# One core, attention and two feed-forward blocks in float32: Strassen's scheme for the first batch and for y, w1 and w2 gone through once

## The chip, the cores and the metric

The kernel runs on one core of one Trainium2 chip. The metric is the device time of one execution in microseconds, the median of three runs. A core has TensorE (PE, with its weight loads as PEld), VectorE (DVE), ScalarE (ACT), GpSimd (POOL) and SyncE (SP), which here issues every DMA. A profiled execution gives the trace from which all rows below are taken.

## What is computed

Four batches of 576 tokens, eight heads of 64, go through three blocks, one after the other:

```python
def _attn_ref(q, k, v):            # window 128, causal, a slope per head
    scores = np.where(mask, scale * np.matmul(q, k.transpose(0, 1, 3, 2)) + bias[None], -1000000000.0)
    attn = softmax(scores)
    return np.matmul(attn, v)

def _moe_ref(x, w1, w2, w3, w_out):   # x 2304x512, w1, w2 512x1024, w3 1024x1024, w_out 1024x512
    a = x @ w1
    b = x @ w2
    h = a * b @ w3
    return h @ w_out

def _moe2_ref(x, w_in, w_out):        # w_in 512x2048, w_out 2048x512
    h = np.maximum(x @ w_in, 0.0)
    return h * h @ w_out
```

## The kernel before

**A planner orders everything.** The kernel consists of tasks (`add(name, rank, where, fn, deps, takes, gives)`), each a few instructions, with an assumed cost on each engine that may run it. `Plan.run` goes through an assumed time: among the tasks that can start within 0.1 us of the earliest it takes the one with the lowest rank, and puts it at the end of its engine's list. So the order on every engine, SyncE's DMA queue among them, is fixed when the kernel is built. `hold` describes a tile: a tag with so many buffers (the table at line 288) and how many tasks must give it back. Gates (tasks of cost 0) close one pool of memory and open another.

**Precision.** A float32 matmul is done as three fast ones: every operand is split into a high and a low part (a copy, and a difference on VectorE or POOL), and `mm3` (lines 194 to 197), `mm3s` and `add_sab` (1080 to 1082) multiply high by high, high by low and low by high. The weights come in as words of 64 bits; `conv_g`, `conv_s`, `conv_m` (lines 328 to 348) turn 1024 of them per partition into float32: a Prelu on ScalarE, a shift on VectorE or ScalarE, a shift with OR on VectorE.

**Strassen's scheme.** Where it is used, a product of 2 x 2 blocks takes seven block products (P1 to P7) in place of eight. Four sums of blocks are made of each operand (`combine`), then seven high and low parts; the seven products accumulate in three PSUM banks, from which VectorE and ScalarE take four results.

**The stages.**
- Attention: sixteen pairs of heads, `add_pair`. Beside it TensorE multiplies w3 by w_out (`p_w34`, L659, 128 matmuls of 512 columns) once and for all, so that y = (a b) w34. The w1, w2 words of eight blocks `fi` of 128 columns are converted (`add_weights`), split for batch 0, and stored in `m_scr["c"]`.
- Batch 0 (`NS = 1`), plain: `add_ab` makes a and b (L195 to L197, output from x and wu), `l_gf` multiplies them to g, `l_gh` and `l_gl` split g, and `add_y` multiplies by w34 (output from gt and wu). The x of batch 0 stays on the chip.
- Batches 1 to 3: x was stored in `x_scr` and is loaded back; `add_xops` makes Strassen's seven operands of it, `add_wmake` loads a block of w1, w2 from `m_scr["c"]` and makes its seven (18 times in all: 8, 5 and 5, since three blocks are kept from batch to batch), `add_sab` makes a, b and g of one block of one batch: 42 matmuls of 288 columns. Then `add_y`, plain, 192 matmuls a batch, from g on the chip; the result goes to `y_scr`.
- r: y by w_in with ReLU, Strassen, 24 groups of 42 matmuls of 384 columns (`add_r`), results to `s_scr`.
- o: squares by w_out, Strassen, nine groups of 168 matmuls of 256 columns (`add_o`), results to `out`.

The words of w_in and w_out of the second block are converted between these (`add_merge`, sixteen of them) and stored in `m_scr`, from where `add_words2` takes them.

## Time and profile before

| | |
|---|---|
| median of three runs | 819.62 us (817.3, 819.62, 821.97) |
| span of the profiled execution | 817.3 us |
| TensorE matmuls | 6724, busy 802.8 us |
| VectorE | 1368 instructions, busy 614.4 us |
| ScalarE | 999 instructions, busy 466.5 us |
| POOL | 69 instructions, busy 57.8 us |
| DMA | 143.99 MB |

Busy times are unions of what an engine shows as running. Matmuls are pipelined, so their busy time says less than their starts do. An idle time is put down to what ended it. A line number can be that of a helper (L200 and L260 are copies on ScalarE and VectorE, L203 is the difference that makes a low part); then the tiles tell what was done.

### The profile page before, as it was taken

Reading aid. Unit: us, or ns where it says so; the run is one execution under the profiler, and the core shown is the slowest. Engines: PE = TensorE matmul, PEld = TensorE weight load, DVE = VectorE, ACT = ScalarE, POOL = GpSimd, SP = SyncE. Lnnn points to the kernel's source line nnn. Section 1 sums busy time; section 2 is a strip of 40 time slices with the busy share of each in tenths; the row PEclk is TensorE's granted clock in tenths of the full one; section 3 lists DMA queues with packets and bytes.
Section 4 is the critical chain, followed back from the end, with each engine's and each line's share of the span. In section 5 each row is a group of like instructions: output and inputs, shape, how many; then the busy total and the mean of one; then the engine's idle time right before and its main releaser. Section 6 shows DMA issues by size and latency. Waiting matters only on the chain. (4 is left out here: it accounts for less than half of the span.)

```text
span 817.3 us, 17269 instructions
## 1 busy us (share of the span) xinstructions
PE 802.8 (98%) x6724; PEld 746.9 (91%) x6724; DVE 614.4 (75%) x1368; ACT 466.5 (57%) x999; POOL 57.8 (7%) x69
## 2 busy tenths in 40 slices
PE   8999999999999999999999999999999999999998
PEld 6665666599999899999999999999999999999998
DVE  6999999956798996896499475733766897667762
ACT  6998888723233442341244476755786785566531
POOL 1000000000001000110040130000222100000000
PEclk9999999999999999999999999999999999999999
DMA  9998989788623642102132457666873755554200
GB/s 224 279 312 262 274 279 279 274 314 263 216 84 109 205 173 84 68 16 84 44 112 101 160 183 263 235 221 210 246 239 134 224 148 155 143 151 135 85 27 33
DMA packets 98402, 143.99 MB, mean 176 GB/s; under 512 B 11024, under 2 KB 75024, under 8 KB 96272
## 3 DMA queue, kind: packets, MB, share of 16 engines
q1 hardware_dynamic: 98320, 142.90, 55.1%
q8 instruction: 52, 0.85, 0.4%
q14 instruction: 30, 0.25, 0.1%
HBM read 98.44 MB, written 44.43 MB: 175 GB/s over the span
## 5 line engine op out<-in xcount | busy, mean ns | idle before, releaser
L196 PE MATMUL g<-gt,wu 128*128 128x288 f32 x256 | 75.7, 296 | 0.0
L195 PE MATMUL g<-gt,wu 128*128 128x288 f32 x256 | 75.6, 295 | 0.0
L197 PE MATMUL g<-gt,wu 128*128 128x288 f32 x256 | 75.4, 295 | 0.0
L443 ACT ACTIVATE e<-e,st 128x128 f32<-128x128 f32 (+1 forms) x144 | 62.3, 435 | 9.0 <-DVE st L435 8.6
L659 PE MATMUL g<-raw 128*128 128x512 f32 x128 | 62.9, 599 | 1.1 <-DVE wu L203 1.0
L200 ACT ACTIVATE D<-xa 128x384 f32<-128x384 f32 (+1 forms) x99 | 45.1, 455 | 30.4 <-PE xa L1133 26.6
L1192 DVE TENSOR_TENSOR D<-xb,D 128x384 f32<-128x384 f32 (+1 forms) x62 | 32.2, 520 | 38.3 <-PE xb L1133 19.0
L1080 PE MATMUL al<-x,wc 128*128 128x288 f32 x192 | 57.5, 299 | 1.1 <-ACT d L200 1.1
L1082 PE MATMUL al<-x,wc 128*128 128x288 f32 x192 | 56.7, 295 | 0.0
L1081 PE MATMUL al<-x,wc 128*128 128x288 f32 x192 | 56.6, 295 | 0.0
L200 ACT ACTIVATE ye<-g 128x288 f32<-128x288 f32 x32 | 13.1, 411 | 73.4 <-PE g L197 66.0
L203 DVE TENSOR_TENSOR ww<-fq,ww 128x1024 fp32r<-128x1024 f32 x35 | 42.5, 1222 | 16.2 <-ACT ww L200 15.9
L200 ACT ACTIVATE ww<-fq 128x1024 fp32r<-128x1024 f32 x35 | 36.9, 1057 | 25.6 <-PE xb L1133 12.0
L1264 ACT ACTIVATE D<-D 128x384 f32<-128x384 f32 x73 | 37.5, 522 | 23.4 <-DVE D L1192 22.4
L868 DVE TENSOR_TENSOR st<-st 128x256 f32<-128x256 f32 (+1 forms) x105 | 41.2, 427 | 9.6 <-DMA st<-m_scrc 5.6
L196 PEld LDWEIGHTS g<-gt,wu 128*128 128x128 f32 x256 | 48.3, 189 | 0.0
L197 PEld LDWEIGHTS g<-gt,wu 128*128 128x128 f32 x256 | 48.2, 188 | 0.0
L195 PEld LDWEIGHTS g<-gt,wu 128*128 128x128 f32 x256 | 48.1, 188 | 0.0
L200 ACT ACTIVATE d<-al 128x288 f32<-128x288 f32 x71 | 28.8, 410 | 32.1 <-PE al L1082 22.9
L503 PEld LDWEIGHTS t<-ident,e 128*128 128x128 f32 x208 | 23.7, 142 | 22.8 <-ACT pt L200 9.7
L435 DVE CUSTOM_DVE_ANT_0 e<-s,bw 128x192 f32<-128x192 f32 (+1 forms) x128 | 40.5, 351 | 1.0 <-PE s L467 0.7
L467 PEld LDWEIGHTS s<-qk 64*64 64x64 f32 x768 | 28.3, 137 | 13.6 <-issue 5.8
(287 smaller groups left out, 2790.9 us busy)
## 6 DMA issues: line engine op xcount, KB each, us to landing
s_scr<-D SPq DMA_DIRECT2D x96, 192.0 KB, 2.1
u<-in_w2io_dram SPq DMA_DIRECT2D x32, 512.0 KB, 6.4
fo<-s_scr SPq DMA_DIRECT2D x20, 512.0 KB, 5.4
qk<-in_qk_dram SPq DMA_DIRECT2D x32, 288.0 KB, 5.5
st<-m_scrc SPq DMA_DIRECT2D x18, 512.0 KB, 3.9
raw<-in_w3t_dram SPq DMA_DIRECT2D x8, 1024.0 KB, 10.2
raw<-in_w_dram SPq DMA_DIRECT2D x8, 1024.0 KB, 7.4
fq<-s_scr SPq DMA_DIRECT2D x16, 512.0 KB, 5.2
```

The costliest lines, as they stand in the source:

```text
L195: nc.tensor.matmul(o, wh, xh, start=start, stop=False)
L196: nc.tensor.matmul(o, wh, xl, start=False, stop=False)
L197: nc.tensor.matmul(o, wl, xh, start=False, stop=stop)
L200: nc.scalar.activation(out=o, in_=i, func=ACTF.Copy)
L203: eng.tensor_tensor(out=o, in0=a, in1=b, op=ALU.subtract)
L435: nc.vector.tensor_tensor_reduce(out=part_of(m, x, rows), in0=ps, in1=bias, op0=ALU.add, op1=ALU.min, scale=-0.125, scalar=3.0e38, accum_o ...
L443: nc.scalar.activation(out=e, in_=e, func=ACTF.Exp, bias=st[:, 0, x:x + 1], scale=-1.0, accum_out=st[:, 1, x:x + 1],)
L659: nc.tensor.matmul(gw[fi], wl, wr, start=c == 0, stop=c == 7)
L868: ENG[e].tensor_tensor(out=o, in0=a, in1=b, op=op)
L1080: nc.tensor.matmul(o, wh, xh, start=start and c == 0, stop=False, skip_group_check=True)
L1081: nc.tensor.matmul(o, wh, xl, start=False, stop=False, skip_group_check=True)
L1082: nc.tensor.matmul(o, wl, xh, start=False, stop=c == 1, skip_group_check=True)
```

## The change

- All sixteen pairs of attention store x in `x_scr`. All four batches are loaded back, and the operands of all four (28 tiles of 576 columns, high and low) are on the chip at the same time, in three pools: xA (open from the start: batch 0 and one of batch 1), xB (open when all of attention's x is stored, gate "sp"), xC (open when w3 w_out is stored, gate "gp").
- w1, w2 are converted and combined once per block. The loop goes over pairs of blocks, in them over the batches, in those over the two blocks. `m_scr["c"]` and the eighteen remakes are gone.
- Batch 0 goes through `add_sab` like the others. The first a, b product waits for "pp": all of x copied out of PSUM.
- g goes to `g_scr` in DRAM (two stores per block and batch), w3 w_out to `w_scr`.
- y is a stage behind a, b, by Strassen's scheme: `add_wy` loads w3 w_out and makes its seven operands of 1024 columns, `add_gops` loads g of one batch (four loads) and makes its seven (in halves of 576 columns), `add_y` does 84 matmuls of 288 columns for each batch and half of the outputs. `add_seven` is the scheme shared with a, b.
- All sixteen `add_merge` are tied to a, b blocks, from the fourth on. Working tiles of r and o (st, s0, fo, yB and the operands of P1, P2) become xA, whose eight tiles have 1152 columns.

```diff
-RANK = dict(w34=3, vv=20, w0=-15, c0=0, cj=3, h0=-40, w12=35.93, w12s=7.96, w12l=7.68, mg=500, mgs=4, yl=8, yn=0, hs=7)
+RANK = dict(w34=3, vv=20, w0=-15, c0=0, cj=3, h0=-40, hs=7, w12=60, wa=7, wl=9, wb=0, x0=20, mg=4, mgs=1.6, wo=1126, gg=-3, yq=1142)
...
-            u=11, u34=4, wo=4, qk=2, v=2, e=NE, s=NPS, t=1, pt=NE, a=5 - NPS, g=2, asb=2, gf=2, gt=8, ye=2,
-            al=2, be=2, ga=2, d1=2, d2=2, d4=2, gq=8, pl=1, xm=1, xt1=1, xt2=1, yA=14, yB=6, s0=1, t2a=1, t2b=1, v6=6, st=2, xa=2, xb=2, xc=2, D1=2, D2=2, D4=2, D3=1, fo=4, fq=5, ww=4,
-            **{f"x_{k}": 1 for k in range(7)},
+            u=11, wo=4, qk=2, v=2, e=NE, s=NPS, t=1, pt=NE, a=5 - NPS, g=2, pl=1, sg=2,
+            d1=2, d2=2, d3=1, d4=2, xA=8, xB=12, xC=8, xa=2, xb=2, xc=2,
+            yA=14, t2a=1, v6=6, D1=2, D2=2, D4=2, D3=1, E1=2, fq=5, ww=4,
...
-    def l_w34h(fi, e):
-        if fi % 2 == 0:
-            w34[fi // 2] = slot("u34")
-        copy(e, w34_part(fi)[:, 0], gw[fi])
-
-    def l_w34l(fi, e):
-        s = w34_part(fi)
-        sub(nc.vector, s[:, 1], gw.pop(fi), f(s[:, 0]))
+    def l_w34(fi, e):
+        t = su.tile([128, 512], F32, tag="sg", bufs=2, name="sg")
+        copy(e, t, gw[fi])
+        gw[fi] = t
+
+    def t_w34(fi):
+        nc.sync.dma_start(out=w_scr[fi], in_=gw.pop(fi))
...
+    def open_pp():
+        psb.close()
+        q = late.enter_context(tc.tile_pool(name="ps_p", bufs=1, space=PSUM, reuse_waits="tile"))
+        pool.update(xa=q, xb=q, xc=q)
...
+    def open_sp():
+        att.close()
+        pool["xB"] = xbs.enter_context(tc.tile_pool(name="xB", bufs=1, side="right", reuse_waits="tile"))
...
+        pool["xC"] = xcs.enter_context(tc.tile_pool(name="xC", bufs=1, reuse_waits="tile"))
+
+    def open_q1():
+        xbs.close()
+        q = q1.enter_context(tc.tile_pool(name="q1", bufs=1, side="right", reuse_waits="tile"))
+        pool.update(yA=q, t2a=q, D1=q)
+
+    def open_ph():
+        xcs.close()
+        dds.close()
+        q = late.enter_context(tc.tile_pool(name="ph", bufs=1, reuse_waits="tile"))
+        pool.update({k: q for k in ("v6", "E1", "D2", "D3", "D4")})
...
+        key = ("w12", fi)
+        add_words(key, rank - RANK["wa"], "u", 8, 3, RANK["wl"] - RANK["wa"], after)
...
+    XA = {(0, P): "xA" for P in SP_}
+    XA.update({(1, P): "xA" if P == 1 else "xB" for P in SP_})
+    XA.update({(2, P): "xC" if P == 4 else "xB" for P in SP_})
+    XA.update({(3, P): "xC" for P in SP_})
+    ROOM = {"xA": [], "xB": ["sp"], "xC": ["gp"]}
...
+        add("lx" + z, rank - 3, {"dma": w_dma(1180)}, lambda e: ld(), [f"sx{4 * b + k}" for k in range(K1)] + prev, ["xm0" + z, "xm1" + z], keep=1)
...
+    def add_seven(z, tag, mms, w, deps, gives, rank, last, y):
...
+        for x, (P, nm, start, dep) in enumerate((
+            (1, "xa", True, []), (2, "xc", True, []), (6, "xa", False, ["d1" + K]), (7, "xb", True, []),
+            (5, "xa", False, ["d2" + K]), (3, "xa", False, ["d4" + K]), (4, "xb", False, ["c22" + K]),
         )):
-            part = A_AT[P][0]
-            add(f"sP{P}_{z}", 1000 + rank + 0.1 * x, {"pe": 6 * w_mm(HALF)}, lambda e, P=P, nm=nm, start=start: prod(P, nm, start),
-                [f"xol{P}_{b}", f"wl{part}c{fi}{w0}"] + [d for d in dep] + ([f"sP1_{last}"] if P == 1 and last else [])
-                + {6: [f"sP1_{z}"], 5: [f"sP6_{z}"], 3: [f"sP5_{z}"], 4: [f"sP7_{z}"]}.get(P, []),
-                take, [f"xo{b}{P}", f"w{part}c{fi}{w0}"])
+            add(f"{tag}{P}_{z}", 1000 + rank + 0.1 * x, {"pe": w}, lambda e, P=P, nm=nm, start=start: prod(P, nm, start),
+                deps(P) + dep + ([f"{last}"] if P == 1 and last else [])
+                + {2: [f"{tag}1_{z}"], 7: [f"{tag}1_{z}"], 6: [f"{tag}1_{z}"], 5: [f"{tag}6_{z}"], 3: [f"{tag}5_{z}"], 4: [f"{tag}7_{z}"]}.get(P, []),
+                [nm + K] if start else [], gives(P))
...
+            add("c12" + K, -20, w_copy(HALF, True), lambda e: cp("d3", e), [f"{tag}3_{z}"], ["d3" + K], ["xa" + K])
+            for nm, c in D.items():
+                add(f"sy{c}{z}", -15, {"dma": w_dma(147)}, lambda e, nm=nm, c=c: y(c, sb.pop((K, nm))), [f"c{c}{K}"], [], [nm + K])
...
+        add_seven(
+            z, "sP", mms, 6 * w_mm(HALF), lambda P: [f"xol{P}_{b}", f"wl{A_AT[P][0]}c{fi}", "pp"],
+            lambda P: [f"xo{b}{P}", f"w{A_AT[P][0]}c{fi}"], rank, last, None,
+        )
...
+        def st(hf, nm):
+            nc.sync.dma_start(out=g_scr[b][fi][:, HALF * hf:HALF * hf + HALF], in_=sb.pop((K, nm)))
+
+        for hf, nm in ((0, "d2"), (1, "d4")):
+            add(f"sg{b}{hf}{fi}", -15, {"dma": w_dma(147)}, lambda e, hf=hf, nm=nm: st(hf, nm), [f"g{hf}{z}"], [], [nm + K])
...
+    def add_wy(rank):
+        for i in range(2):
+            hold(f"ym{i}", "u", 100)
+        hold("ysx", "xA", 6)
+
+        def ld(i):
+            t = wm[i] = new("u", [128, 4, 512])
+            nc.sync.dma_start(out=t, in_=w_scr[4 * i:4 * i + 4].rearrange("k p n -> p k n"))
+
+        for i in range(2):
+            add(f"lw{i}", rank - 3, {"dma": w_dma(1048)}, lambda e, i=i: ld(i), [f"sw{4 * i + k}" for k in range(4)] + ([f"lw{i - 1}"] if i else [f"whbc{NF1 - 1}"]), [f"ym{i}"], keep=0)
+        M = lambda i: wm[i % 2][:, :, 256 * (i // 2):256 * (i // 2) + 256]
+
...
+    GA = {(b, P): (("xB" if P in (1, 2, 6, 7, 5, 3) else "xA") if b % 2 == 0 else "xC" if P in (1, 2, 6, 7) else "xB" if b == 1 else "xA") for b in range(B) for P in SP_}
...
+        for x, i in enumerate((0, 1, 3, 2)):
+            add(f"lg{i}{z}", rank - 1 + 0.1 * x, {"dma": w_dma(590)}, lambda e, i=i: ld(i),
+                [f"sg{b}{i % 2}{fi}" for fi in range(4 * (i // 2), 4 * (i // 2) + 4)] + ([f"gc3_{b - 1}"] if b else []), [f"gm{i}{z}"])
...
+        for i, (dp, tk, gv) in enumerate((
+            (["lg0" + z, "lg1" + z], [s0], [m[0], m[1]] + [s0]), (["gc0" + z, "lg3" + z], [s1], [m[3], s0, s1]),
+            (["gc0" + z, "lg3" + z], [], [m[1], m[3]]), (["gc1" + z, "lg2" + z, "gl50" + z, "gl51" + z], [], [m[2], s0, s1]),
+        )):
+            add(f"gc{i}{z}", rank + (0, 0.1, 0.2, 0.5)[i], w_tt(4 * HALF), lambda e, i=i: combine("B", i, M, S_, e), dp, tk, gv)
...
+            return [
+                (*(wy[P][:, h, k, 128 * c:128 * c + 128] for h in range(2)), *(go[b, P, k // 2][:, h, k % 2] for h in range(2)))
+                for k in range(4)
+            ]
...
+    add("pp", 0, {"gate": 0.0}, lambda e: open_pp(), [f"xh{g_}_{m}" for g_ in range(2) for m in range(4 * B)])
+    add("sp", 0, {"gate": 0.0}, lambda e: open_sp(), [f"sx{m}" for m in range(4 * B)])
+    add("gp", 0, {"gate": 0.0}, lambda e: open_gp(), [f"sw{i}" for i in range(NF1)])
+
     g = 100
-    order = list(range(NF1))
-    at_w = {}
+    last = None
+    sabs = []
     for b in range(B):
-        if b < NS:
-            for hf in range(2):
-                for i in range(NF1):
-                    add_ab(b, hf, i, g)
-                    g += 1
-                for i in range(K1):
-                    add_y(b, hf, i, g + (hf and RANK["yl"] * (i >= RANK["yn"])))
-                    g += 1
-            continue
-        FO[b] = order
-        at_w[b] = order[-NKEEP:]
-        order = order[:-NKEEP - 1:-1] + order[:-NKEEP]
-    last = None
-    g0 = g
-    for b in range(NS, B):
-        made = b == NS
-        if made:
-            prev = []
-        prev_x = [f"xol{P}_{b - 1}" for P in SP_] if b > NS else []
-        add_xops(b, 1000 + g0 + 20 * (b - NS) - 13, prev_x)
-        for x, fi in enumerate(FO[b]):
-            r = 1000 + g + 1.5 * x
-            kept = b + 1 < B and fi in at_w[b]
-            if b > NS and fi in at_w[b - 1]:
-                w0 = b - 1
-            else:
-                w0 = b
-                add_wmake(fi, b, 1 + kept, r - 6, prev)
-                prev = [f"whbc{fi}{b}"]
-            add_sab(b, fi, g, w0, last)
-            last = f"{b}{fi}"
-            g += 1
-        for i in range(K1):
-            for hf in range(2):
-                add_y(b, hf, i, g + RANK["yl"] * (i >= RANK["yn"] and b < B - 1))
+        add_xops(b, 1000 + g + 2 * b - RANK["x0"], [f"xc3_{b - 2}"] if b > 1 else [])
+    for p in range(NF1 // 2):
+        for x in range(2):
+            add_wmake(2 * p + x, 1000 + g + x - 6, B, [f"sP1_{RANK['wb'] + x}{2 * p - 2}"] if p > 1 or p and x else [])
+        for b in range(B):
+            for x in range(2):
+                add_sab(b, 2 * p + x, g, last)
+                last = f"sP1_{b}{2 * p + x}"
+                sabs.append(last)
                 g += 1
+    add_wy(RANK["wo"])
+    for b in range(B):
+        add_gops(b, 1000 + g + RANK["gg"] + 4 * b)
+    for b in range(B):
+        for c in range(2):
+            add_y(b, c, g, last)
+            last = f"Y1_{b}{c}"
+            g += 2
...
+    add("q1", 0, {"gate": 0.0}, lambda e: open_q1(), [f"Y{P}_{b}1" for b in range(lb) for P in SP_ if GA[b, P] == "xB"])
+    add("ph", 0, {"gate": 0.0}, lambda e: open_ph(),
+        [f"sy{k}{lb}{c}" for k in ("11", "12", "21", "22") for c in range(2)] + [f"Y{P}_{lb}1" for P in SP_])
...
+        add_merge(k, m, 1080 + x, prev + [sabs[min(31, int(RANK["mg"] + RANK["mgs"] * x))]])
```

## Rows read from the trace of the kernel before

**Rows 1.** Busy times by stage: window, length, engine busy (instructions), clock, DMA share, GB/s.

```profile
0.00:160.80 160.80, 153.66 (x1988) 101.50 (x1988) 144.30 (x598) 135.62 (x438) 5.53 (x22) 0.99 0.91 273
167.00:456.00 289.00, 285.83 (x2132) 283.35 (x2133) 227.44 (x449) 103.68 (x203) 23.33 (x19) 1.00 0.38 130
```

In the order PE, PEld, DVE, ACT, POOL.

**Rows 2.** Timeline of TensorE: start, duration, line, output and inputs.

```profile
166.71 0.22 PE L543 MATMUL a<-pt,v 64*64 64x64 f32 x1
166.86 0.40 PE L195 MATMUL g<-x,wu 128*128 128x288 f32 x1
...
454.07 0.29 PE L197 MATMUL g<-gt,wu 128*128 128x288 f32 x1
...
456.46 0.29 PE L197 MATMUL g<-gt,wu 128*128 128x288 f32 x1
456.59 0.34 PE L1131 MATMUL xa<-yA,u 128*128 128x384 f32 x1
...
457.12 0.34 PE L1131 MATMUL xa<-yA,u 128*128 128x384 f32 x1
```

**Rows 3.** Busy times in slices of 20 us, columns as in rows 1.

```profile
280.00:300.00 20.00, 19.38 (x142) 18.89 (x142) 19.58 (x37) 11.62 (x20) 1.45 (x1) 1.00 0.35 132
...
340.00:360.00 20.00, 19.57 (x145) 19.09 (x144) 19.17 (x40) 10.93 (x23) 6.19 (x5) 1.00 0.01 5
...
380.00:400.00 20.00, 20.00 (x153) 20.00 (x152) 10.79 (x20) 5.54 (x12) 0.00 (x0) 1.00 0.20 65
```

**Rows 4.** Groups of instructions up to 165 us; then tiles wu and x there.

```profile
L345 DVE SCALAR_TENSOR_TENSOR raw<-raw 128x1024 uint32<-128x1024 uint32 x20 | 24.4, 1222 | 0.5
L339 DVE TENSOR_SCALAR raw<-raw 128x1024 uint32<-128x1024 uint32 x16 | 10.9, 693 | 0.1
L200 ACT ACTIVATE pt<-t 128x512 f32<-128x512 f32 x46 | 27.2, 592 | 9.1 <-PE t L503 8.0 <-ACT e L443 1.0
L330 ACT ACTIVATE raw<-raw 128x1024 f32<-128x1024 f32 x20 | 23.1, 1160 | 0.0
L200 ACT ACTIVATE pt<-a 128x256 f32<-128x256 f32 (+1 forms) x33 | 8.4, 324 | 1.1 <-PE a L543 1.1
...
0.00:165.00 165.00, 3.55 (x24) 3.24 (x24) 20.09 (x23) 5.84 (x9) 0.99 0.91 273
...
0.00:165.00 165.00, 3.55 (x24) 3.24 (x24) 3.53 (x12) 3.00 (x12) 0.99 0.91 273
```

A group has its count, busy time, mean duration in ns, and the idle time before it with what ended that. The windows of a tile have PE, PEld, DVE, ACT.

**Rows 5.** Groups of instructions from 167 to 456 us; then tiles wc and gt there.

```profile
L868 DVE TENSOR_TENSOR st<-st 128x256 f32<-128x256 f32 x72 | 27.5, 419 | 6.0 <-DMA st<-m_scrc 5.6
L1103 DVE TENSOR_TENSOR d<-be,d 128x288 f32<-128x288 f32 x48 | 21.5, 453 | 4.3 <-ACT d L200 2.7 <-PE be L1082 1.3
L203 DVE TENSOR_TENSOR gt<-d,gt 128x288 fp32r<-128x288 f32 x39 | 16.9, 455 | 1.0
L1109 DVE TENSOR_TENSOR d<-d,d 128x288 f32<-128x288 f32 x23 | 12.2, 534 | 0.7
L203 DVE TENSOR_TENSOR x<-xm,x 128x576 fp32r<-128x576 f32 x12 | 8.8, 751 | 0.0
L203 POOL TENSOR_TENSOR gt<-d,gt 128x288 fp32r<-128x288 f32 x9 | 7.8, 870 | 49.3 <-DVE gt L260 32.5 <-ACT gt L200 16.8
L200 ACT ACTIVATE x<-xm 128x576 fp32r<-128x576 f32 x11 | 7.3, 681 | 1.1 <-PE al L1082 0.8 <-PE be L1082 0.3
...
167.00:456.00 289.00, 140.34 (x1008) 135.58 (x1008) 48.08 (x53) 13.98 (x16) 7.84 (x3) 1.00 0.38 130
...
167.00:456.00 289.00, 105.34 (x764) 102.77 (x765) 38.36 (x98) 8.32 (x19) 7.78 (x9) 1.00 0.38 130
```

**Rows 6.** DMA up to 165 us in all; issues with size and time to landing.

```profile
DMA packets 22150, 44.98 MB, mean 273 GB/s; under 512 B 6261, under 2 KB 12405, under 8 KB 20076
...
s_scr<-D SPq DMA_DIRECT2D x96, 192.0 KB, 2.1
```

**Rows 7.** Waits of ScalarE from 637 us to the end: total, times, longest.

```profile
ACT fq L1305 <- DMA fq<-s_scr: 10.6, 10, 2.1
```

More of the change, by code (lines that the diff above doesn't have):

```diff
@@ L206, in fused_kernel @@
     y_scr = dram.tile([K1, 128, NT], F32, name="y_scr")
+    g_scr = [dram.tile([NF1, 128, S], F32, name=f"g_scr{b}") for b in range(B)]
+    w_scr = dram.tile([NF1, 128, DM], F32, name="w_scr")
     TN = 384
@@ L755, in p_y @@
-    def p_y(b, hf, oi, part):
-        if part == 0:
-            yo[b, hf, oi] = ps_g.tile([128, 512], F32, tag="g", name="g")[:, 0:HALF]
-        o = yo[b, hf, oi]
-        fs = (FO[b] if b >= NS else range(NF1))[4 * part:4 * part + 4]
-        for x, fi in enumerate(fs):
-            w = w34[fi // 2][:, :, (fi % 2) * 512 + oi * 128:(fi % 2) * 512 + (oi + 1) * 128]
-            g = gt[b, hf, fi]
-            mm3(o, w[:, 0], w[:, 1], g[:, 0], g[:, 1], part + x == 0, part == 1 and x == 3)
-    def l_y(b, hf, oi, e):
-        t = gp[0].tile([128, HALF], F32, tag="ye", bufs=2, name="ye")
-        copy(e, t, yo[b, hf, oi])
-        yo[b, hf, oi] = t
@@ L796, in fused_kernel, with new @@
+    def new(tag, shape, dt=F32):
+        return (wp if tag == "u" else pool[tag]).tile(shape, dt, tag=tag, bufs=plan.caps[tag], name=tag)
     A_AT = {1: "a0", 2: "a1", 3: "b2", 4: "a3", 5: "b0", 6: "b1", 7: "a2"}
@@ L1005, in hi @@
             def hi(e, part=part, w=w, o=o):
[L1006 to L1007 removed]
+                t = wc[fi, part] = new("u", [128, 2, w], F32R)
+                copy(e, t[:, 0], full()[:, o:o + w])
             def lo(e, part=part, w=w, o=o):
[L1010 to L1013 removed]
@@ L1070, in prod @@
         def prod(P, nm, start):
             if start:
-                sb[z, nm] = ps_p[0].tile([128, 512], F32, tag=nm, bufs=plan.caps[nm], name=nm)[:, 0:HALF]
-            o = sb[z, nm]
-            part = A_AT[P][0]
-            i = 256 * int(A_AT[P][1])
-            w, x = wc[fi, w0, part], xo[b, P]
-            for c in range(2):
-                wh, wl = (w[:, h, i + 128 * c:i + 128 * c + 128] for h in range(2))
-                xh, xl = (x[:, h, HALF * c:HALF * c + HALF] for h in range(2))
+                sb[K, nm] = new(nm, [128, 512])[:, 0:HALF]
@@ new lines, in add_y, with mms, y @@
+    def add_y(b, c, rank, last):
+        z = f"{b}{c}"
+        def mms(P):
+            return [
+                (*(wy[P][:, h, k, 128 * c:128 * c + 128] for h in range(2)), *(go[b, P, k // 2][:, h, k % 2] for h in range(2)))
+                for k in range(4)
+            ]
+        def y(k, t):
+            i, h = int(k[0]) - 1, int(k[1]) - 1
+            t0 = b * S + h * HALF
+            nc.sync.dma_start(out=y_scr[c + 2 * i, :, t0:t0 + HALF], in_=t)
+        add_seven(
+            z, "Y", mms, 12 * w_mm(HALF), lambda P: [f"gl{P}{q}_{b}" for q in range(2)] + [f"ywl{P}"],
+            lambda P: [f"go{b}{P}{q}" for q in range(2)] + [f"wy{P}"], rank, last, y,
+        )
@@ L1356, in prod @@
             return ([f"ol{P}{t}"] + [f"wl{part}o{m}" for m in range(NM)],
-                    [f"ow{P}{t}"] + [f"w{part}o{m}" for m in range(NM)], lambda o, start, P=P, **kw: p_o(t, P, o, start, **kw))
+                    owns[t, P] + [f"w{part}o{m}" for m in range(NM)], lambda o, start, P=P, **kw: p_o(t, P, o, start, **kw))
         def fin(z):
```

596 lines of the change are left out of this document (267 added, 329 removed).

## Prediction

> **What bounds the kernel now.** I read the table of stages first [rows 1]. Up to 160.8 us (attention, with w3 w_out on the side) VectorE is busy 144.3 us (0.90), ScalarE 135.6 us (0.84), and DMA has a share of 0.91. TensorE's 153.7 us there are pipelined latencies and mislead, as the next view shows. From 167 to 456 us TensorE is busy 285.8 of 289 us and VectorE only 227.4 (0.787). So there are two regimes: an attention stage that VectorE and ScalarE set, and then 650 us that TensorE sets.
>
> The second view is the timeline of TensorE [rows 2]. Its starts tell what a matmul of 288 columns costs: 454.07 to 456.46 is eighteen intervals, 0.132 us each, not the 0.30 us that one lasts. The last P V product of attention starts at 166.71, the first matmul of the r stage at 456.59. Between them lie 2136 of the 2160 matmuls of 288 columns that the code has (384 for a, b of batch 0, 1008 for Strassen's a, b, 768 for y); the other 24 have run inside attention, in tile wu of [rows 4]. 2136 x 0.132 = 282.0 of 289.7 us, so the holes are 7.7 us. By slices of 20 us [rows 3]: where VectorE works 10.8 us, 153 matmuls fit; where it works 19.2 or 19.6 us, 145 or 142. A dense VectorE costs TensorE some nine matmuls, 1.2 us in 20.
>
> **The change part by part.** All working is on the profiled span of 817.3 us; the median of the runs is 819.6, so 2.3 is added at the end.
>
> *Matmuls.* By the code, batch 0 goes from 2 x 8 x 2 x 12 = 384 to 8 x 42 = 336, and y from 4 x 2 x 4 x 24 = 768 to 4 x 2 x 84 = 672: 144 fewer of one width, 19.0 us. After the end of attention 2016 stand in place of 2136: 120 x 0.132 = -15.8 us (the other 24 ran inside attention, which the next term contains).
>
> *Attention stage.* Off it go, of VectorE: eight of the OR steps (9.8), eight shifts (5.5), everything into wu (20.1: high and low parts of w1, w2, low parts of w3 w_out) and the low parts of x (3.5) [rows 4], 38.9 us; of ScalarE eight Prelu steps and one copy, 10.3. On it comes what the first products of a, b need. The operands of x for batch 0 are four sums and seven differences at 0.75 us and seven copies at 0.68 [rows 5]: 8.3 and 4.8 us. Three sums and one operand of batch 1 (it lies in xA) are 3.0 and 0.7. A block of w1, w2 costs VectorE 0.69 + 1.22 + 4 x 0.42 + 1.22 + 0.92 = 5.7 us and ScalarE 1.16 + 1.16 + 0.87 = 3.2 (the parts of 768 scaled from 1024) [rows 4, 5]; two of them are 11.5 and 6.4. VectorE goes from 144.3 to 128.2, ScalarE from 135.6 to 137.2; their sum from 279.9 to 265.4, a factor of 0.948, which puts the end of attention from 166.9 to 158. Without the added work the factor is 230.7 / 279.9 = 0.824: 138 us. The added work has the later rank, so attention runs ahead of it, but it must be there before the first product: I take 152 us (-14.9). DMA forbids little more: 45.0 MB [rows 6] less 14.7 (w1, w2 in and back out, four w2io loads) plus 7.8 (more of x out, x in for two batches, w3 w_out out, two blocks in) is 38.1 MB, at 273 GB/s 140 us, the lower bound. Upper bound: 167, if the chain of a pair of heads and not the engines sets the pace.
>
> *Gates.* The new products wait for "pp", all of x copied out of PSUM, where the old ones waited for batch 0 alone. The last three copies take 0.32 us of ScalarE each [rows 4], and their semaphores: +1.5 us (0 if w3 w_out has matmuls left to cover it, 5 if the first weights are late too). The operands in xB wait for "sp", the stores of x; a store lands in some 2.1 us [rows 6], and batch 1 is due only two blocks (84 x 0.132 = 11 us) later: covered. On SyncE's queue 90 transfers are new (64 stores and 16 loads of g, 10 for w3 w_out); a store whose g is late holds the loads of weights behind it, and TensorE waits for those.
>
> *VectorE between attention and r.* Away: 40 of 72 sums for w1, w2 (16.8), of the 48.1 us into wc all but sixteen differences (31.0), everything into gt (38.4), fifteen products a b of batch 0 at 0.45 (6.8) [rows 5]: 93.0 us. To it: eight more blocks of a, b with four additions or products at 0.45 and one at 0.53 (18.8), words of w1, w2 (15.3), 24 additions for y at 0.45 (10.9), eleven steps of 1024 for w3 w_out (13.4), five w2io conversions that now come early (9.6), and the operands of g, four times four sums of 1152 (1.37, scaled from 1.22 for 1024) and 14 differences of 576 (0.75): 64.0 us. Together 132.0. Less what is made in attention (two blocks 11.5, batch 1's 3.0), VectorE goes from 227.4 to 251.9 us. TensorE needs 2016 x 0.132 = 266.1, so VectorE's share rises from 0.79 to 0.95 of that: every slice is a dense one. Fourteen slices at 1.2 us are 16 us of holes in place of 7.7: +8 us (0 if POOL and ScalarE take the surplus; 20 if the joints stall too).
>
> *Joints.* From a, b to y: before its first seven products are through, y needs all operands of w3 w_out and those of g for batch 0. Both can begin when the last block of batch 0 is done, six blocks (33 us) before the end, and VectorE has 14.1 us of a, b, 13.4 and 16 us to do: 43.5 us of work in 33 + 11 us. It fits with nothing over, and is within the +8. From y to r: "ph" waits for the last y store (2.1 us); products 1, 2, 6, 7 of the first r block, 24 matmuls that start every 0.176 us [rows 2], 4.2 us, cover it. In r and o no matmul changes; the five w2io conversions only leave.
>
> *Sum:* 817.3 - 14.9 - 15.8 + 1.5 + 8.0 = 796.1, and with 2.3 for the median **798 us**.
>
> **The rivals.**
> *Attention not shortened.* It ends at 167 because pairs are bound by their chain. For: ScalarE keeps its 137 us. Against: ScalarE's idle time is 9.1 us, put down to transposes, ahead of the copies behind them [rows 4], and VectorE is at 0.90. 798 + 15 = 813.
> *Short attention, no new holes.* It ends at 140, and VectorE keeps up: 798 - 12 - 8 = 778. For: VectorE's work fits into 266 us. Against: the slices of rows 3.
> *POOL is no relief.* The planner may hand differences of g, x and the weights to POOL. For: POOL takes 0.87 us for the difference that VectorE does in 0.455, and VectorE's product out of SBUF has a mean of 0.534 against 0.453 for the sums that read PSUM [rows 5]: handing over 20 differences gives VectorE 9 us and, if it is held meanwhile, takes up to 17, so that the holes grow by 8 more: 806. Against: POOL does only 19 steps in this stretch now [rows 1]. The Trainium skill, "SBUF — State Buffer", section "SBUF: two separate sides", has this as a rule: the two share a port pair as an exclusive lock, and a VectorE instruction with two SBUF inputs is held for the whole of a POOL instruction that reads SBUF. By that rule the sum is 806, without it 798; no row here shows one instruction held by another.
> *Slower: VectorE takes the bound between attention and r.* It must then wait at each joint for g's way through DRAM, as it waits for TensorE now. At its present density of 0.787 the 251.9 us last 320 us; r would begin at 152 + 1.5 + 320 = 473.5 instead of 456.6, 17 us late: 837. It decides from a density below 251.9 / 303.1 = 0.83. For: every difference of g now stands behind the store of its last f block and a load. Against: in attention VectorE holds 0.90, and in two slices of rows 3 0.96 and 0.98.
> *The o stage starves.* Its loads and operands leave pools of their own (fo, st) for xA, eight tiles of which a step takes six, so that loads start later. ScalarE's longest wait for such a load is 2.1 us now, and covered [rows 7]. If each of eight steps lost 2.1 us: 798 + 17 = 815.
>
> **How the numbers follow.** Forecast (790 to 805) 0.38; short attention without holes 0.18; attention not shortened 0.14; POOL 0.08; o starves 0.08; slower 0.14. A measurement of this kernel tells 0.5% (4.1 us) from no change. Below 815.5 us lie the first four and a little of the fifth: faster 0.79; the rest of the fifth and the lower edge of the slower case: same 0.08; slower 0.13. The range, 779 to 816, takes in the bounds of attention and of the holes one at a time, and leaves out the slower case and the corner of the fast one where both ends meet.
>
> **What would show it.** Right: the last P V product near 152 us; 2016 matmuls of 288 columns from there to the first of 384 columns, in some 282 us, at 0.132 each; VectorE above 0.88 there; r to the end still 361 us. Wrong: P V ending at 165 or later; TensorE waiting above 5 us at "pp", before the first y product or before r; VectorE's sums waiting for loads of g; r and o together longer than 365 us.

## The result, and the profile after

| | before | after |
|---|---|---|
| median (lowest to highest) | 819.62 us (817.3 to 821.97) | 806.28 us (804.9 to 812.59) |
| ratio, 95% interval | | 0.9848 [0.9807, 0.9889] |
| span of the profiled execution | 817.3 us | 810.8 us (of 812.59) |

The change is faster by 1.5%. Forecast were 798 us and faster; 806.3 lies inside the range, 8 us above the forecast. The profiled execution is the longest of its kernel, so a second profile of the kernel after (a_again, below) stands beside it. Three stretches answer to the three terms of the sum; their ends are read from TensorE's timeline.

| | before | after | difference | a_again | difference | forecast |
|---|---|---|---|---|---|---|
| start to last P V product | 166.71 | 167.70 | +1.0 | 165.42 | -1.3 | -14.9 |
| to the last matmul of 288 columns | 289.75 | 275.21 | -14.5 | 276.24 | -13.5 | -6.3 |
| to the end | 360.84 | 367.89 | +7.1 | 365.74 | +4.9 | 0 |
| sum | 817.3 | 810.8 | -6.5 | 807.4 | -9.9 | -21.2 |

The middle forecast is -15.8 + 1.5 + 8.0. That the time still lies inside the range is in part luck, since errors of opposite sign stand in the sum: attention got hardly shorter, the holes that were feared did not come, and r and o, for which nothing was forecast, got longer.

Busy times by stage, after (columns as in [rows 1], which they answer):

```profile
0.00:167.70 167.70, 159.03 (x2046) 106.35 (x2046) 132.71 (x571) 142.16 (x462) 12.19 (x25) 0.96 0.83 249
167.80:438.80 271.00, 266.96 (x1996) 264.50 (x1993) 233.75 (x374) 146.03 (x263) 25.46 (x17) 1.00 0.69 223
```

VectorE did lose work in attention, 144.3 to 132.7 us, but the stage didn't end earlier. Between attention and r VectorE's share rose from 0.787 only to 0.863, not to 0.95. The timeline of TensorE after, which answers [rows 2]:

```profile
167.69 0.22 PE L513 MATMUL a<-pt,v 64*64 64x64 f32 x1
167.84 0.40 PE L929 MATMUL xa<-xA,u 128*128 128x288 f32 x1
...
437.22 0.29 PE L929 MATMUL xa<-xA,u 128*128 128x288 f32 x1
...
438.68 0.30 PE L931 MATMUL xa<-xA,u 128*128 128x288 f32 x1
438.81 0.34 PE L1125 MATMUL xa<-yA,u 128*128 128x384 f32 x1
...
442.91 0.29 PE L931 MATMUL xb<-xA,u 128*128 128x288 f32 x1
443.04 0.34 PE L1125 MATMUL xc<-yA,u 128*128 128x384 f32 x1
```

The first product of a, b starts 0.15 us after the last P V product, as it did before [rows 2]: the gate "pp" costs nothing. From 437.22 to 438.68 lie eleven intervals of 0.133 us, the price of a matmul as before. Six matmuls of r run ahead of the last 24 of y. So in the 275.2 us stand 2016 x 0.1327 = 267.5 and 1.1 for the six, and 6.6 us of holes; before, 2136 x 0.1328 = 283.7 of 289.75, 6.1 of holes.

### The profile page after: what moved, and what is told of

Same layout as the page of the kernel before. It is cut to its first block, busy times and chain, and to the rows that moved or that the text cites. A ratio compares the mean times of both kernels' runs of the same rounds, so it can differ in the third digit from the quotient of the medians.

```text
span 810.8 us, 17310 instructions
## 1 busy us (share of the span) xinstructions
PE 791.7 (98%) x6582; PEld 735.0 (91%) x6582; DVE 612.7 (76%) x1291; ACT 510.7 (63%) x1090; POOL 67.9 (8%) x65
## 5 line engine op out<-in xcount | busy, mean ns | idle before, releaser
L196 ACT ACTIVATE d<-xa 128x288 f32<-128x288 f32 x128 | 52.2, 409 | 97.4 <-PE xa L931 93.3
L196 ACT ACTIVATE D<-xa 128x384 f32<-128x384 f32 (+1 forms) x91 | 41.8, 462 | 30.0 <-PE xa L1127 26.4
L931 PE MATMUL xa<-xB,u 128*128 128x288 f32 x192 | 56.8, 296 | 0.0
L929 PE MATMUL xa<-xB,u 128*128 128x288 f32 x192 | 56.8, 296 | 0.0
L930 PE MATMUL xa<-xB,u 128*128 128x288 f32 x192 | 56.1, 292 | 0.0
L716 DVE TENSOR_TENSOR xA<-xA 128x256 f32<-128x256 f32 (+2 forms) x74 | 47.7, 669 | 3.0 <-DMA xA<-g_scr 1.5
L950 DVE TENSOR_TENSOR d<-xb,d 128x288 f32<-128x288 f32 x80 | 36.2, 452 | 15.2 <-ACT d L196 10.8
L473 PEld LDWEIGHTS t<-ident,e 128*128 128x128 f32 x208 | 24.4, 144 | 23.6 <-ACT pt L196 11.2
L437 PE MATMUL s<-qk 64*64 64x128 f32 (+2 forms) x768 | 37.5, 293 | 5.0 <-issue 2.1
L473 PE MATMUL t<-ident,e 128*128 128x128 f32 x208 | 36.8, 291 | 1.7 <-ACT pt L196 1.3
L930 PEld LDWEIGHTS xa<-xB,u 128*128 128x128 f32 x192 | 36.5, 190 | 0.0
L929 PEld LDWEIGHTS xa<-xB,u 128*128 128x128 f32 x192 | 36.1, 188 | 0.0
L931 PEld LDWEIGHTS xa<-xB,u 128*128 128x128 f32 x192 | 36.0, 188 | 0.0
L1127 PE MATMUL xa<-yA,v 128*128 128x384 f32 x104 | 35.2, 339 | 0.0
```

The lines of the kernel that those rows point to most:

```text
L196: nc.scalar.activation(out=o, in_=i, func=ACTF.Copy)
L437: nc.tensor.matmul(HD[2 * m + r]["s"][g][o, c:c + w], t[h, 0, 64 * q:64 * q + 64], t[h, 1, 64 * k:64 * k + w], start=True, stop=True,)
L473: nc.tensor.transpose(o, e[:, u:u + 2, :].rearrange("p u c -> p (u c)"), ident)
L716: ENG[e].tensor_tensor(out=o(oi), in0=a(ai), in1=b(bi), op=op)
L929: nc.tensor.matmul(o, wh, xh, start=start and c == 0, stop=False, skip_group_check=True)
L930: nc.tensor.matmul(o, wh, xl, start=False, stop=False, skip_group_check=True)
```

## The experiments

Each changes the kernel after, or, where it says so, a version of that. What a kernel leaves out stands with it.

**The two kernels again**, unchanged.

> The changed kernel as it is, a second profile. In the first one attention ended at 167.7 us, with the granted clock at 0.83 from 40 to 60 us, and the span was 810.8; other executions had spans of 803 to 806 at a mean clock of 0.996 to 0.998. Theory A (the lower clock cost those microseconds): a profile with a mean clock of 0.996 or more has P V ending at 158 to 162 and the rest as before, span 803 to 806. Theory B (attention is no shorter, and the differences lie elsewhere): P V ends at 166 to 168 whatever the clock.

> The kernel before as it is, on the same chip as the run of the changed kernel beside it, for two numbers of its profile. In the first profiles the matmuls of the o stage started every 0.1182 us before and every 0.1200 after, 3 us over 1512. If that is the chip, both kernels now show the same interval; if it is the layout of the changed kernel, 0.1182 here and 0.1200 there. P V is expected to end at 165 to 168.

The kernel after: 810.19 us (0.9885 [0.9836, 0.9934]); before: 819.81. The last P V product came at 165.42 in the one and at 167.47 in the other, so that neither theory for a_again holds as it stands. The granted clock in the first profile of after was 0.93 and 0.83 in the slices 20 to 40 and 40 to 60 us, in this one 1.00 and 0.91. That is 4.8 and 1.8 us of full speed lost, which leaves 162.9 and 163.6 (an estimate; the first 20 us, at 0.90 and 1.00, are left out of it). The clock can explain why the two profiles differ, not why both are over 10 us from 152. The interval of o's matmuls is taken up in the last section.

**Fillers up to 95 us.** The planner puts small transposes into TensorE's idle times, so far up to 40 us of assumed time.

```diff
-    FILL = 40.0
+    FILL = 95.0
```

> The changed kernel with filling matmuls allowed into planned idle time of TensorE up to 95 us instead of 40 us (the constant FILL); no result changes. Theory A (a drop of the granted clock between 20 and 60 us costs attention time): no slice below 0.97, P V ends at 158 to 161, time 802 to 805 with less spread than the 804.9 to 812.6 of the changed kernel. Theory B (the clock there does not matter to attention's end): the changed kernel's time within 2 us, or some more, for the fillers stand in TensorE's queue.

808.04 us (0.9858 [0.9832, 0.9884]): no change, and the edit made none. The trace has the same instructions on every engine as that of after, with the same 46 small matmuls by `ident`. So this run tests neither theory; it is a third measurement of the kernel after. Its last P V came at 164.2, with the clock at 1.00 and 0.91 in the two slices as in a_again: one program differs by 1.3 us there at the same clock.

**Attention's added work held back.** The loads of x operands and of w1, w2 wait until all of x is out of PSUM.

```diff
-        add_words(key, rank - RANK["wa"], "u", 8, 3, RANK["wl"] - RANK["wa"], after)
+        add_words(key, rank - RANK["wa"], "u", 8, 3, RANK["wl"] - RANK["wa"], ["pp", *after])
...
-        add("lx" + z, rank - 3, {"dma": w_dma(1180)}, lambda e: ld(), [f"sx{4 * b + k}" for k in range(K1)] + prev, ["xm0" + z, "xm1" + z], keep=1)
+        add("lx" + z, rank - 3, {"dma": w_dma(1180)}, lambda e: ld(), [f"sx{4 * b + k}" for k in range(K1)] + ["pp"] + prev, ["xm0" + z, "xm1" + z], keep=1)
```

> The changed kernel with the conversion of the first blocks of w1, w2 and the loads of x for Strassen's operands held back until attention's x is all copied out; the result stays. Off attention go some 11 us of ScalarE and 26 of VectorE. Theory A (VectorE and ScalarE set attention's pace, as the prediction had it): P V ends at 138 to 148 instead of 163 to 168. Theory B (TensorE, with w3 w_out beside attention, or the chain of a pair sets it): P V ends at 158 to 166. In both TensorE then waits 15 to 30 us for the first operands, so that the time as a whole says nothing.

851.85 us. Up to the last P V product, now at 160.85, VectorE was busy only 108.7 us and ScalarE 130.8. Slices of 20 us, then TensorE's timeline:

```profile
100.00:120.00 20.00, 20.00 (x271) 13.06 (x273) 9.73 (x59) 16.77 (x60) 0.00 (x0) 1.00 0.59 170
...
140.00:160.00 20.00, 20.00 (x238) 12.83 (x238) 8.64 (x48) 14.20 (x49) 0.00 (x0) 1.00 0.28 98
```

```profile
161.00 4.56 PE L613 MATMUL g<-raw 128*128 128x512 f32 x10
201.92 0.61 PE L929 MATMUL xa<-xA,u 128*128 128x288 f32 x1 [36.36 <-ACT u L196]
```

VectorE at 0.49 and 0.43, DMA at 0.59 and 0.28, and still no faster: Theory B, and this falsifies the forecast's picture of the stage. TensorE is the one column at 20.00. The two lines of the timeline show more: ten w3 w_out products are left over, and with them TensorE's work of the stage ends at 165.6, where that of a_again ended at 165.4. Then TensorE stands for 36 us, which is what the early work is worth.

**Half of the w3 w_out products left out** (so w3 w_out, and the output with it, is another).

```diff
-        nc.tensor.matmul(gw[fi], wl, wr, start=c == 0, stop=c == 7)
+        if c % 2 == 0:
+            nc.tensor.matmul(gw[fi], wl, wr, start=c == 0, stop=c == 6)
```

> The changed kernel without half of the products w3 by w_out (every second block of the sum is left out; loads and conversions stay), which takes 64 matmuls of 512 columns, 27 us, off TensorE's work in attention and nothing off the other engines. Theory A (TensorE plays no part in attention's pace): P V ends at 162 to 167 as before. Theory B (TensorE is one of the engines that set it): P V ends at 145 to 158.

805.68 us, the last P V at 161.74, between the two theories and nearer to A. That alone would say that TensorE doesn't set the pace; but the slices show another state of the stage:

```profile
40.00:60.00 20.00, 16.52 (x181) 10.95 (x173) 15.72 (x70) 17.73 (x59) 0.00 (x0) 0.83 0.80 254
60.00:80.00 20.00, 17.12 (x194) 10.09 (x192) 16.37 (x55) 15.60 (x45) 0.00 (x0) 0.83 0.76 251
...
120.00:140.00 20.00, 18.77 (x322) 13.23 (x322) 16.81 (x85) 19.52 (x68) 1.41 (x1) 1.00 1.05 281
140.00:160.00 20.00, 16.57 (x207) 10.15 (x206) 19.55 (x67) 18.80 (x59) 2.29 (x3) 1.00 0.46 153
```

TensorE, with gaps, was given a clock of 0.83 for 40 us (6.8 us lost), and later ScalarE (19.52) and VectorE (19.55) are full. So the 28 us that were taken away (64 products at 0.44 us) were covered by the next limit and by a lower clock; the run doesn't tell how much by each.

**Two PSUM banks for the transposes**, taken from the scores' three.

```diff
-NPS = 3
+NPS = 2
...
-    ps_t = psb.enter_context(tc.tile_pool(name="ps_t", bufs=1, space=PSUM))
-    ps_v = psb.enter_context(tc.tile_pool(name="ps_v", bufs=5 - NPS, space=PSUM))
+    ps_t = psb.enter_context(tc.tile_pool(name="ps_t", bufs=2, space=PSUM))
+    ps_v = psb.enter_context(tc.tile_pool(name="ps_v", bufs=2, space=PSUM))
```

> PSUM in attention is divided anew: the transposes of the scores get two banks in place of one, the scores two in place of three; nothing else is changed by hand (the planner orders attention anew). Theory A: the chain score, transpose, copy, P V through the one bank of transposes sets the pace of attention (ScalarE's longest idle time there is put down to transposes): the last P V product falls from 164 to 168 us to 158 or earlier, and the whole becomes 800 or less. Theory B: the chain runs over the scores' banks or over the exchange between VectorE and ScalarE, and this buffer doesn't matter: the last P V stays at 162 or later, and later than 168 if the scores now lack a bank.

832.53 us. The last P V came at 161.1, between the two theories; but 28 products of w3 w_out (161.28 to 173.00) were still to do, and a, b began at 173.0, later than in after. The second bank of transposes, at the price of one of the scores', didn't shorten the stage.

**Most of the conversion of w3, w_out left out**, on the version nopool (below); the output isn't the reference's.

```diff
+        if key[0] in ("w3", "wo"):
+            add("cn" + k, rank, {"D": 0.66}, lambda e: conv_s(key, e), ["ld" + k])
+            return
         add("cg" + k, rank, w_act(1024), lambda e: conv_g(key), ["ld" + k])
```

> On the version without POOL in sums and differences: of the conversion of the twelve tiles of w3 and w_out only the shift on VectorE (0.69 us) is left; the Prelu on ScalarE (1.14 us) and the shift with OR on VectorE (1.23 us) are left out, 13.7 us of ScalarE and 14.8 of VectorE in the first 100 us, so w3 w_out, and with it the output, is not the reference's. TensorE's and the DMA's work stays. The planner orders attention anew. Theory A: the lists of VectorE and ScalarE set attention's pace together: the last P V product falls from 161.1 by what the busier loses, to 147 to 150. Theory B: the chain of a pair, or the loads, set it: 157 to 162. (Attention's added work held back had left it at 160.9, with VectorE at 108.7 us of work and ScalarE at 130.8.)

806.04 us, the last P V at 159.6: Theory B. Of 160 us VectorE was busy 118.9 and ScalarE 128.0. A slice, then TensorE's timeline inside it:

```profile
60.00:80.00 20.00, 20.00 (x213) 11.61 (x212) 7.34 (x34) 10.60 (x36) 0.00 (x0) 1.00 0.92 296
```

```profile
62.34 0.66 PE L476 MATMUL t<-ident,e 128*128 128x128 f32 x4
62.84 1.02 PE L616 MATMUL g<-raw 128*128 128x512 f32 x2
63.79 1.11 PE L440 MATMUL s<-qk 64*64 64x128 f32 x32
64.83 0.65 PE L476 MATMUL t<-ident,e 128*128 128x128 f32 x4
...
67.73 0.88 PE L440 MATMUL s<-qk 64*64 64x192 f32 x16
68.54 1.98 PE L616 MATMUL g<-raw 128*128 128x512 f32 x4
...
74.12 1.24 PE L500 MATMUL a<-pt,v 128*64 128x192 f32 x28
75.29 0.51 PE L516 MATMUL a<-pt,v 64*64 64x64 f32 x18
...
75.92 1.12 PE L616 MATMUL g<-raw 128*128 128x512 f32 x2
76.88 0.60 PE L476 MATMUL t<-ident,e 128*128 128x128 f32 x4
77.32 3.60 PE L616 MATMUL g<-raw 128*128 128x512 f32 x8
80.85 1.11 PE L440 MATMUL s<-qk 64*64 64x128 f32 x32
```

With VectorE at 0.37 and ScalarE at 0.53, every row of TensorE begins before the row ahead of it ends: it never stands. The starts give prices: a w3 w_out product 0.44 us (eight from 77.32 to 80.85), four transposes 0.50, a pair's scores 1.04 + 0.81, a pair's P V 1.80 (74.12 to 75.92). In all: 128 x 0.44 + 208 x 0.124 + 16 x 1.85 + 16 x 1.80 = 56.3 + 25.8 + 29.6 + 28.8 = 140.5 us, and with some 10 us for the start (first matmul at 3.60, thirty small transposes of some 0.2) an estimate of 150 us below which this attention can hardly end. In the kernels before and after it is the same picture. Groups of TensorE from 60 to 160 us, first after, then before (columns as in [rows 4]):

```profile
L613 PE MATMUL g<-raw 128*128 128x512 f32 x104 | 51.4, 602 | 0.0
L473 PE MATMUL t<-ident,e 128*128 128x128 f32 x134 | 22.6, 282 | 0.0
L437 PE MATMUL s<-qk 64*64 64x192 f32 (+2 forms) x448 | 19.9, 281 | 0.1
```

```profile
L659 PE MATMUL g<-raw 128*128 128x512 f32 x104 | 51.0, 599 | 1.0 <-DVE wu L203 1.0
L503 PE MATMUL t<-ident,e 128*128 128x128 f32 x134 | 22.7, 282 | 0.0
L467 PE MATMUL s<-qk 64*64 64x128 f32 (+2 forms) x432 | 18.9, 280 | 0.6 <-DVE st L435 0.6
```

Idle in 100 us: 0.1 and 1.6.

**No sums and differences on POOL.**

```diff
-    def w_tt(n, engs="Dp"):
+    def w_tt(n, engs="D"):
...
-    def w_ts(n, engs="Dap"):
+    def w_ts(n, engs="Da"):
```

> The changed kernel with POOL taken out of the choice for all elementwise steps, so that VectorE does what POOL did (some 40 steps, 50 us of POOL's time, 21 us by VectorE's own prices). Theory A (POOL's steps hold VectorE for as long as they run, two of VectorE's differences of 512 columns lasted 1.75 us instead of 0.69 beside one of POOL): the time is within 2 us of the changed kernel's 805 to 810, or less, and the wait at the start of o shrinks. Theory B (POOL relieves VectorE): 5 us or more slower.

802.64 us, 0.9798 [0.9768, 0.9829]: Theory A, and below both kernels, though its interval overlaps that of after in part. Its stage from a, b to r, then groups of VectorE in it; behind them the groups of after in its own stage:

```profile
162.60:435.40 272.80, 268.21 (x1994) 264.76 (x1993) 233.34 (x396) 146.93 (x260) 0.00 (x0) 1.00 0.68 225
```

```profile
L981 DVE TENSOR_TENSOR d<-d,d 128x288 f32<-128x288 f32 x32 | 14.6, 457 | 1.0
...
L199 DVE TENSOR_TENSOR u<-u 128x1024 fp32r<-128x1024 f32 x7 | 8.4, 1218 | 1.4 <-ACT u L196 1.4
```

```profile
L981 DVE TENSOR_TENSOR d<-d,d 128x288 f32<-128x288 f32 x32 | 18.0, 563 | 1.0
...
L199 DVE TENSOR_TENSOR u<-u 128x1024 fp32r<-128x1024 f32 x7 | 9.7, 1394 | 0.0
```

POOL's 25.5 us and 17 steps are gone, VectorE has 22 instructions more, and is busy 233.3 us as against 233.75. The product out of SBUF takes 457 ns in place of 563 (534 in [rows 5]), a difference 1218 in place of 1394. POOL's help was taken back in full. The stage isn't shorter for it. The last P V product came at 161.06, at a clock of 1.00 all through, but four w3 w_out products were left over:

```profile
161.21 1.98 PE L613 MATMUL g<-raw 128*128 128x512 f32 x4
```

So a, b began at 162.63, against 165.57 in the second profile of after: 2.9 us gained, of which 1.8 can be the clock. From there to the last of 288 columns nopool loses 0.8 us, and behind it it gains 3.6.

**Product 2's operand earlier in the first step of o.**

```diff
-    turn = ["Q1o0", "P1o0", "Q2o0", "P2o0", "P4o0", "P6o0", "P7o0", "P5o0"]
+    turn = ["Q1o0", "Q2o0", "P1o0", "P2o0", "P4o0", "P6o0", "P7o0", "P5o0"]
```

> The changed kernel with one pair of the first o step swapped: product 2 over the first six blocks before product 1 over the last two. In the changed kernel's profile TensorE waits 0.5 and 1.6 us at 624 to 627 us for the last block of w_out, and its clock is lower until 631 us. Theory A (the operands of product 2 lie ready and 18 matmuls, 2.2 us, cover the wait): 3 to 4 us faster than the changed kernel. Theory B (product 2's operands are as late): no change. The interval of 0.120 us between matmuls of o stays in both.

805.51 us (0.984 [0.9805, 0.9875]): Theory B. In after, TensorE's longest wait behind r was `xa` for VectorE's `u`, 1.6 us; here it is the next operand:

```profile
PE xc L1127 <- DVE ww L199: 2.4, 1, 2.4
```

The wait moves to what VectorE makes last; so VectorE's list at this joint, and not the order of products, holds TensorE up. Attention ran at a clock of 1.00 here, and the last P V came at 163.1.

**VectorE loaded more between attention and r.** First three, then one (`range(1)`) extra operation of 288 columns, 0.45 us, in each of the 32 blocks of a, b; the output is unchanged.

```diff
+            for _ in range(3):
+                nc.vector.tensor_tensor(out=sb[K, "d4"], in0=sb[K, "d4"], in1=sb[K, "d4"], op=ALU.max)
```

> The changed kernel with three more VectorE instructions (288 columns, out of SBUF, 0.45 us each; the larger of a value and itself, so that nothing changes) in each of the 32 blocks of a, b: 43 us more on VectorE, of which 234 of 271 us are used between attention and r. Theory A (VectorE has only the 37 us that it shows idle): a, b to r lasts 285 us or more. Theory B (VectorE was never near the bound there, since much of its work has early deadlines only in the plan): 272 to 278 us.

> One extra VectorE operation of 128x288 (0.45 us) in each of the 32 block products a, b, 14.4 us in all, so that VectorE's load between attention and r becomes some 248 us, near the 251.9 that the forecast assumed. Theory A (the forecast's rule of dense slices): TensorE loses 1.2 us per dense slice, the stretch from the first product of a, b to r goes from 271 to 272 us up to 278 to 280. Theory B (VectorE is just below its bound as its list is ordered, and nearly every added us is paid; 43 us more cost 39.5): up to 284 or more. Theory C (there are 37 us of idle VectorE, and 14 fit in): 271 to 274.

845.74 and 810.79 us. The stretch from the first product of a, b to r, first of dve3, then of dve1:

```profile
164.70:476.20 311.50, 280.11 (x1996) 271.08 (x1993) 281.31 (x452) 151.40 (x267) 65.75 (x37) 0.98 0.59 193
```

```profile
164.70:440.30 275.60, 267.70 (x1996) 264.63 (x1993) 248.24 (x402) 149.65 (x267) 39.52 (x24) 1.00 0.66 219
```

dve3 is Theory A. VectorE's density is 281.31 / 311.5 = 0.903 and 248.24 / 275.6 = 0.901. That it is the same in both speaks for 0.90 as VectorE's ceiling in this stretch, as the planner orders it, and for dve1 standing at it (both have more on POOL as well, 65.75 and 39.52 us): 14.5 us more work, 3.6 to 4.6 us more time (271.0 and 272.0 in the two profiles of after). dve1 fell between A and C of its expectation. The kernel after, at 0.863, is below the ceiling: 233.75 / 0.901 = 259.4 us, less than TensorE's 267.5.

**A third of attention's transposes copied by VectorE**, on nopool.

```diff
-            add(f"pt{g}_{m}", rj + 1, w_copy(128 if g == 3 else 512, True), lambda e, g=g: l_pt(m, g, e),
+            add(f"pt{g}_{m}", rj + 1, ({"d": 0.64} if g == 1 else w_copy(128 if g == 3 else 512, True)), lambda e, g=g: l_pt(m, g, e),
```

> On the version without POOL in sums and differences: of the three copies of 512 columns that a pair of heads makes from the bank of transposes (0.59 us each, ScalarE's in the kernels so far), the second goes to VectorE by rule, sixteen in all, 9.4 us; the planner orders attention anew. In that version ScalarE is busy 138.5 of the 161.1 us up to the last P V product, VectorE 131.8; with attention's added work held back, VectorE fell to 108.7, ScalarE only to 130.8, and the last P V still came at 160.9. Theory A: ScalarE's list sets attention's pace: its load falls to some 129 us, the last P V product comes near 152 us (161.1 less 9.4), and the whole becomes 793 to 796. Theory B: the chain of a pair (scores, row maxima, exponentials, transposes, copies, P V) sets the pace, whichever engine copies: the last P V stays between 158 and 163, and the whole between 800 and 806. Theory C: VectorE's list decides, and the copies lengthen it: later than 164.

814.18 us (0.9948 [0.9931, 0.9965]): Theory C. The last P V came at 167.6, and from 100 us on VectorE is full, in the end with gaps on TensorE:

```profile
100.00:120.00 20.00, 20.00 (x260) 12.91 (x260) 19.36 (x80) 18.59 (x62) 0.00 (x0) 1.00 1.00 280
120.00:140.00 20.00, 19.99 (x253) 12.01 (x252) 19.57 (x78) 17.83 (x57) 0.00 (x0) 1.00 0.82 244
140.00:160.00 20.00, 18.03 (x239) 11.56 (x241) 19.60 (x77) 17.88 (x57) 0.00 (x0) 1.00 0.58 182
```

So VectorE is close behind TensorE there: with these copies, some ten us, on its list it takes over. The amount alone doesn't decide it: the kernel before had 143.5 us on VectorE up to 160 us, more than the 138.7 here, and TensorE stayed all but full. That these copies stand in the way of P V itself is a likely reason, not tested.

## Why the prediction was right or wrong

**What bounds attention: wrong, and with it the largest term.** The step that failed is the sentence that TensorE's 153.7 us "are pipelined latencies and mislead", so that VectorE and ScalarE set the stage. For a matmul of 288 columns the record is twice the interval (0.30 and 0.13 us), and I carried that to attention without looking at starts there. The starts leave TensorE next to no idle time from 60 us on, before as after. A w3 w_out record lasts 0.60 us, so records overlap even where TensorE waits a little; but from 60 us to the last P V half of the intervals behind such a product are 0.43 us and nine in ten at most 0.53, in both kernels. The Trainium skill, "Perfetto Trace Analysis", section "Identifying the Most-Contended Engine", says that matmul busy time is not a good measure of how close TensorE is to its roofline, and points to the flops reached and to the busy share of weight loads instead; that share is 0.58 to 0.67 in the slices from 60 to 160 us of after, so by it too TensorE looks free. The starts decide. What the change took from TensorE in attention was 24 matmuls, 24 x 0.133 = 3.2 us. The runs agree, as far as the clock can be taken off: after gives 162.9 and 163.6 without the clock's dips, turnq 163.1 at a clock of 1.00, and the two profiles of before, counted alike (0.98 and 0.93 in the slice 20 to 40), 166.3 and 166.1. The term was -14.9; -3.2 is what rows of before would have given.

Shown: TensorE is dense from 60 us to the end of attention; no relief of VectorE, ScalarE, DMA or of the transposes' bank brought the last P V below 159.6 us, and where P V came early, w3 w_out mostly came late (early_off, t2, four products in nopool). What can be won without fewer matmuls lies before 60 us: there TensorE's records leave 8.6 us idle in after, 8.0 in nopool and 4.2 in noconv, and noconv began a, b 2.9 us before nopool. Not shown: which list makes the stage end where it does when TensorE gets less work (w34half). There ScalarE and VectorE reach 19.5 of 20 us late in the stage, and the clock is down for 40 us; that the three limits lie within some ten us of each other fits all runs, but no run separates the clock from the rest. The rival "attention not shortened" has the right result (167) for a wrong reason; its 813 lacks what follows.

**Matmuls: right.** 2016 stand in place of 2136, at 0.133 us as before: -16.

**Gates: within their bounds (0 to 5 us);** the gate cost nothing in place of 1.5 us. VectorE's sums waited 1.5 us in all for loads of g (2.8 in a_again).

**Holes: wrong, mis-sized.** Forecast +8, measured +0.5 (6.6 for 6.1; 7.6 for the second profile, 276.2 - 267.5 - 1.1). The forecast's 7.7 for before came of an interval read as 0.132; 2.39 / 18 is 0.133. The step that failed is VectorE's load of 251.9 us. It began with a busy time (227.4, a union) and added instructions at their durations. Neighbours overlap in the records: durations add up to 249.3 us in the stretch before, and to 255.6 after, where the busy times are 227.4 and 233.75. That is the smaller fault, some 2 us (an estimate from these shares). The larger is the ledger itself: by durations VectorE's load rose by 6.3 us, where the ledger has 132.0 - 93.0 - 14.5 = 24.5. w1, w2 lost 50.6 us in this stage, not 44.0, since a third block was made before a, b began; twenty of the 32 sums are left in after:

```profile
L716 DVE TENSOR_TENSOR raw<-raw 128x256 f32<-128x256 f32 x20 | 7.7, 421 | 0.3
```

The operands of r lost 6.4 us there, for which the ledger has nothing. The rest is smaller, among it seven differences of 576 columns that POOL did. So VectorE's share went from 0.79 to 0.86, not to 0.95. The rule read from [rows 3] was not far off: dve1, with 248.2 us of busy time, has 279.8 - 268.6 = 11.2 us of holes. By that the forecast's load would have cost about what the forecast said, an estimate.

**Joints: the y joint right, r and o wrong.** "In r and o no matmul changes" is true, and still r and o took 4.9 to 7.1 us longer (2.6 in fill95, the same program). Behind r stands a wait that was not there before, and a shorter one early in r. The early one, then TensorE behind r, then VectorE and POOL, all of after:

```profile
PE xb L1125 <- DVE D L1189: 0.7, 1, 0.7
```

```profile
625.03 0.38 PE L1125 MATMUL xa<-u,xA 128*128 128x256 f32 x1 [0.48 <-ACT u L196]
627.04 0.58 PE L1126 MATMUL xa<-u,xA 128*128 128x256 f32 x1 [1.62 <-DVE u L199]
627.42 0.42 PE L1127 MATMUL xa<-u,xA 128*128 128x256 f32 x1
627.63 0.41 PE L1125 MATMUL xc<-u 128*128 128x256 f32 x1
```

```profile
618.44 3.49 DVE L199 TENSOR_TENSOR xA<-xA 128x512 fp32r<-128x512 f32 x2
618.64 2.74 POOL L199 TENSOR_TENSOR u<-xA,u 128x1024 fp32r<-128x1024 f32 x1 [1.09 <-ACT u L196]
619.04 2.89 DVE L199 TENSOR_TENSOR xA<-xA 128x512 fp32r<-128x512 f32 x1
```

Two differences of 512 columns take VectorE 3.49 us while POOL does one of 1024. The last line is the second of the two by itself: the first lasts 0.68 us, the second 2.89, and it ends 0.55 us behind POOL's. VectorE is late from there on, and TensorE waits 0.5 and 1.6 us for its operands. Behind the wait the intervals are 0.21 us (627.42 to 627.63) in place of 0.12: TensorE runs at the lower of its two clocks (granted 0.50 from 627.5 to 630.1 us, after a stretch of 2 us with one matmul), and the slice 620 to 640 us has a granted clock of 0.91, 1.8 us. Without POOL the same two differences take 1.28 us:

```profile
613.66 1.28 DVE L199 TENSOR_TENSOR xA<-xA 128x512 fp32r<-128x512 f32 x2
```

and TensorE's waits there are 0.9 and 0.8 us. In after the waits behind r (2.1), those in r (0.7 and 0.2), the clock (1.8) and o's interval (2.7, last section) make 7.5 us; the six matmuls of r that ran ahead take off 1.1. That leaves 6.4 of the 7.1 us explained.

**POOL is no relief: right as a mechanism, mis-priced as a time.** In the stage for which it was priced at +8 us it cost nothing, since VectorE is below its ceiling. It cost at the joint of r and o. The Trainium skill, "SBUF — State Buffer", section "SBUF: two separate sides", states the lock by which a VectorE instruction with two SBUF inputs waits out a POOL instruction that reads SBUF and began first. The forecast had no row that shows one; here it shows in the difference of 2.89 us that ends just behind POOL's instruction, against 0.68 without POOL, and on average as 563 ns against 457 for the product.

**VectorE takes the bound: not here,** but nearer than it was given credit for. The rival was to decide if VectorE could reach no more than a density of 0.83; it reached 0.90 in dve1 and dve3, and after lies at 0.863. dve1, 14.5 us further, is at it.

**Short attention without holes** had its second half right. **o starves**: no such wait; ScalarE and VectorE made o's operands in time from its second step on.

Of the signs that the forecast named for being wrong, two came: P V ended at 165 or later (167.7 and 165.4), and r and o took more than 365 us (367.9 and 365.7).
